# Making the masks and decays of retention on the chip as outer products, with a new order of the work

## The chip, the core and the metric

One core of a Trainium2 chip runs one program. The core's engines are TensorE (PE, matmuls; PEld is its loading of weights), VectorE (DVE), ScalarE (ACT), GpSimd (POOL) and SyncE (SP, which here issues every DMA). Each runs its own instructions in order and waits on semaphores for the others. The metric is the time of one execution on the device in microseconds (us), the median of several runs; lower is better.

## What is computed

```python
def _attn_ref(q, k, v):                      # q, k, v: (4, 8, 576, 64) float32
    scores = scale * np.matmul(q, k.transpose(0, 1, 3, 2))
    gamma = 1.0 - 2.0 ** (-5.0 - np.arange(H, dtype=np.float32))
    rel = pos[:, None] - pos[None, :]
    Dmat = np.where(rel >= 0, gamma[:, None, None] ** rel[None, :, :], 0.0)
    return np.matmul(scores * Dmat[None, :, :, :], v)

def _moe_ref(x, w_in, w_out):                # x: (2304, 512), d_ff = 2048
    h = x @ w_in
    return (h * np.cos(h)) @ w_out

def _moe2_ref(x, w_in, w_out):
    h = x @ w_in
    return (np.maximum(h, 0.0) + np.log1p(np.exp(-np.abs(h)))) @ w_out
```

Retention (attention with a decay `gamma ** (distance)` per head in place of a softmax), then two dense layers with different activations. Scale is 1/8.

## The kernel before

**Retention.** A sequence of 576 tokens is cut into a first part of 256 and a second of 320. One *piece* is one part of one batch for one pair of heads: 32 pieces. A piece's raw tile `raw` holds queries, keys and values. PE makes the scores of two 128-token blocks (`scores`, line 615) into a set of two PSUM banks (`s`/`o`, `acc0`/`acc1`, `acc2`/`acc3`, `ha`/`hb` in turn), DVE multiplies them by the mask `m_t` (line 642, `p<-s`), POOL scales the keys by `dk_t` (line 585) and the queries by `dq_t` (line 592, `qs`), PE sums keys times values (`sums`, line 620) to a state `st`, and two pieces later PE adds the masked and the carried part (`back`, line 692). `m_t` has a 128x128 triangle per head, `dq_t` a decay by position, `mt_t` the masks of the last 64 tokens. All three were computed on the host and are loaded, as is the small `dk_t`. ACT and DVE then split the result in a high and a low part (`x`, lines 727 and 308).

**The layers.** Every fp32 factor is split in two reduced-precision parts, `gh`/`gl`, `wh`/`wl`, and three products are summed. Weights come as 64-bit words (`wr`) and are rebuilt by ACT (`wy`, `wr`, lines 363 and 369) and DVE (`wk`, lines 375 to 386) before they are split into `wh` and `wl` (line 431 and the helper of line 308). The first 8 of 16 column blocks `f` of layer 1 run in groups of 512 or 384 tokens (lines 779 and 883). From about 278 us on the rest of layer 1 and layer 2 run as a Strassen-like scheme (lines 921 and 1001), in which `tt`, `pair`, `cv` and `x` are sums and differences of blocks.

**What sets the order.** Every operation is given to `Plan.op` with an engine, an estimated duration, a key (a wished time) and its dependences. `Plan.order` then lists them by a model of engines, ports and the DMA link; the model's times decide the order of each engine's instructions, and for operations that may run on two engines (`POOL_DVE`, `ACT_DVE`) also which. Nothing of these times is kept on the chip: only the order and the data's semaphores count. The first 16 pieces (`4 * ALONE`) come alone, the others between matmuls of the first three groups. Ahead of piece 0 and after pieces 0 and 1 PE runs filling matmuls on zeros (`warm`, `fill`, line 1053; `FILL = (2, 5)`).

Of the kernel before, what the change touches and what calls it, by code (L numbers as in the profile page):

```python
# [7 lines left out]
F32 = mybir.dt.float32  # L8
# [46 lines left out]
def t_pool(n):  # L55
    return n * 0.00228 + 0.06
# [9 lines left out]
    return layer == 2 or f < FA  # L66


FLEX = 0.317
FLEX_AD = 0.993  # L70
FLEX_2 = 50.0
ROOM = 258.786
SPARE = 0.082
LATE = 3.0
NP = 3
RS = 5
WR = 3
GB = 2
PT = 3
R0 = 22.0  # L80
WB = (21.627, 3.294)
W2 = (31.803, 7.371, 15.278, -5.922)
W3 = (30.221, 11.772, 18.502)
XC = 9.717
LAG_C = 1.399
LAG_S = 0.9
TT = 3
CA = (-2.626, 2.436, 6.269, 13.332)
TURN = 0.6
XS = 61.276  # L90
FILL = (2, 5)
EARLY = 2.474
EARLY_2 = 5.754
AHEAD = {}
GAP = 2.0
LO_A = "pool or dve"
END = 3.1
LC = 2.5
LL = 3.862
LB = 1.9  # L100
WARM = 350
DX = 20.621
LEAD = 7.302
W0 = (40.929, 1.68, 3.451)
M0 = 28.434
AK = (1.0, 2.2)
# [8 lines left out]
TIE = -0.21
LAG = -2.133
LEAD_G = 7.197
CX = 0.278
# [5 lines left out]
class Plan:  # L124
# [29 lines left out]
    def order(self):  # L154
        n = len(self.ops)
        behind, loose = [set() for _ in range(n)], set()
        for bufs, made in self.rings.values():
            for k, (i, _) in enumerate(made):
                if k:
                    behind[i].add(made[k - 1][0])  # L160
                if k >= bufs:
                    self.ops[i][4].update(self.users.get(made[k - bufs][1], ()))
            for i, tile_key in made:
                for u in self.users.get(tile_key, ()):
                    if u != i:
                        if i not in self.ops[u][4]:
                            loose.add((u, i))
                        self.ops[u][4].add(i)
        for i, o in enumerate(self.ops):
            o[4].discard(i)  # L170
            behind[i].discard(i)
            behind[i] -= o[4]
        after = [[] for _ in range(n)]
        next_ = [[] for _ in range(n)]
        left = [0] * n
        for i, o in enumerate(self.ops):
            left[i] = len(o[4]) + len(behind[i])
            for d in behind[i]:
                next_[d].append(i)
            for d in o[4]:  # L180
                after[d].append(i)
        ready = [0.0] * n
        free, port, link = dict.fromkeys(("pe", "act", "dve", "pool", "sp", "host"), 0.0), 0.0, 0.0
        can = [i for i in range(n) if not left[i]]
        start, end, self.eng = [0.0] * n, [0.0] * n, [None] * n
        window, busy, warm = 0, 0.0, False
        for _ in range(n):
            best = None
            for i in can:
                eng, dur, key, _, _, uses_port, _ = self.ops[i]  # L190
                if eng == POOL_DVE:
                    f = max(ready[i], port)
                    t, d, e = min(
                        ((max(f, free[e]), d, e) for e, d in (("pool", t_pool(dur)), ("dve", t_dve(dur)))),
                        key=lambda o: o[0] + (FLEX if ready[i] < ROOM else FLEX_2) * o[1])
                elif eng == ACT_DVE:
                    t, d, e = min(
                        ((max(ready[i], free[e], port if e == "dve" and uses_port else 0.0), d, e) for e, d in zip(("act", "dve"), dur)),
                        key=lambda o: o[0] + FLEX_AD * o[1] + (SPARE if o[2] == "dve" else 0.0))
                else:  # L200
                    t, d, e = max(free[eng], ready[i], port if uses_port else 0.0, key - LEAD if eng == "sp" else 0.0), dur, eng
# [53 lines left out]


@with_exitstack
def retention_moe_moe(ctx, tc, qkv, w1, w2, mask, mtail, dq, dk, out):
    nc = tc.nc
    pool = lambda name, bufs=1, **kw: ctx.enter_context(tc.tile_pool(name=name, bufs=bufs, **kw))  # L260
    dram = pool("dram", space=bass.MemoryType.DRAM)
# [269 lines left out]
    def front(i, K):  # L531
# [99 lines left out]
    def masks(i, K):  # L631
# [225 lines left out]
    def parts(e, src, r, n, i, K2, in_psum):  # L857
# [211 lines left out]
    HT = ("ha", "hb", "s", "o")

# [254 lines left out]
```

## Time and profile before

| | us |
|---|---|
| median of 3 runs | 858.13 (857.58 to 859.51) |
| the profiled execution | 857.71 |
| its span, first to last instruction | 855.9 |
| PE busy | 842.1 (98%) |
| DVE busy | 653.2 (76%) |
| ACT busy | 480.0 (56%) |
| POOL busy | 53.2 (6%) |

The profiled execution's own time is 1.8 us longer than its span. PE's matmuls overlap in the pipeline, so a busy PE need not be at its peak. An idle engine costs time only where another waits for it.

### The profile page before, as it was taken

Reading aid. Unit: us, or ns where it says so; the run is one execution under the profiler, and the core shown is the slowest. Engines: PE = TensorE matmul, PEld = TensorE weight load, DVE = VectorE, ACT = ScalarE, POOL = GpSimd, SP = SyncE. Lnnn points to the kernel's source line nnn. Section 1 sums busy time; section 2 is a strip of 40 time slices with the busy share of each in tenths; the row PEclk is TensorE's granted clock in tenths of the full one; section 3 lists DMA queues with packets and bytes.
Section 4 is the critical chain, followed back from the end, with each engine's and each line's share of the span. In section 5 each row is a group of like instructions: output and inputs, shape, how many; then the busy total and the mean of one; then the engine's idle time right before and its main releaser. Section 6 shows DMA issues by size and latency. Waiting matters only on the chain.

```text
span 855.9 us, 13829 instructions
## 1 busy us (share of the span) xinstructions
PE 842.1 (98%) x5084; PEld 756.9 (88%) x5084; DVE 653.2 (76%) x1281; ACT 480.0 (56%) x951; POOL 53.2 (6%) x73
## 2 busy tenths in 40 slices
PE   7989999999999999999999999999999999999998
PEld 5767777899988899999999998898998988989986
DVE  3889987776799898778899898588669665655653
ACT  1378654746676776556777575466547533333331
POOL 3630100100121000000000000000000000000000
PEclk9999999999999999999999999999999999999999
DMA  8876779654784132332377658357456454252203
GB/s 311 343 264 202 268 260 353 204 198 157 257 289 157 52 124 95 128 126 80 122 261 263 227 187 331 127 216 273 160 196 227 173 194 158 75 181 78 74 1 111
DMA packets 66852, 160.56 MB, mean 188 GB/s; under 512 B 6240, under 2 KB 26336, under 8 KB 66784
## 3 DMA queue, kind: packets, MB, share of 16 engines
q1 hardware_dynamic: 66784, 159.68, 53.2%
q8 instruction: 40, 0.66, 0.3%
q14 instruction: 28, 0.23, 0.1%
HBM read 104.34 MB, written 55.31 MB: 187 GB/s over the span
## 4 chain that ended last, share of the span: by engine, by line
PE 86%; DVE 7%; ACT 3%; issue 1%; DMA 1%; SPq 0%; POOL 0%; DVEq 0%; POOLq 0%; ACTq 0%
PE acc L1001 34%; PE ha L921 17%; PE acc L883 9%; PE s L921 8%; PE hb L921 4%; PE ha L779 4%; PE hb L779 3%; PE o L692 2%; PE s L615 1%; DVE tt L1175 1%; DVE wk L382 1%; PE s L779 1%; PE s L620 1%; DMA dq_t<-in_dq 1%; DVE gl L308 1%
## 5 line engine op out<-in xcount | busy, mean ns | idle before, releaser
L1001 PE MATMUL acc<-pair,gh 128*128 128x512 f32 x576 | 178.5, 391 | 0.0
L921 PE MATMUL ha<-x,pair 128*128 128x384 f32 x864 | 174.3, 336 | 0.0
L921 PEld LDWEIGHTS ha<-x,pair 128*128 128x128 f32 x864 | 152.6, 188 | 5.1 <-DVE g L831 0.3
L308 DVE TENSOR_TENSOR gl<-g,gh 128x384 fp32r<-128x384 f32 x144 | 79.6, 554 | 66.6 <-ACT gh L862 66.0
L862 ACT ACTIVATE gh<-g 128x384 fp32r<-128x384 f32 x144 | 74.8, 521 | 92.1 <-PE acc L1001 88.4
L1001 PEld LDWEIGHTS acc<-pair,gh 128*128 128x128 f32 x576 | 107.3, 188 | 19.0
L1001 PE MATMUL acc<-pair,gl 128*128 128x512 f32 x288 | 113.3, 393 | 0.0
L1001 PE MATMUL acc<-gh,pair 128*128 128x384 f32 x384 | 105.1, 334 | 0.0
L845 ACT ACTIVATE er<-er 128x384 f32<-128x384 f32 x96 | 50.3, 524 | 73.5 <-DVE er L842 73.0
L921 PE MATMUL s<-x,pair 128*128 128x384 f32 x432 | 86.8, 335 | 0.9 <-DVE gl L308 0.9
L921 PEld LDWEIGHTS s<-x,pair 128*128 128x128 f32 x432 | 75.9, 188 | 1.5 <-DVE gl L308 1.2
L1001 PEld LDWEIGHTS acc<-gh,pair 128*128 128x128 f32 x384 | 70.1, 188 | 0.0
L1001 PE MATMUL acc<-gl,pair 128*128 128x384 f32 x192 | 64.5, 336 | 1.1 <-DVE gl L308 1.1
L828 ACT ACTIVATE er<-er,hp_t 128x384 f32<-128x384 f32 (+1 forms) x88 | 56.3, 643 | 15.5 <-DVE er L825 14.2
L1001 PEld LDWEIGHTS acc<-pair,gl 128*128 128x128 f32 x288 | 54.0, 188 | 11.4
L883 PE MATMUL acc<-gh,wh 128*128 128x512 f32 (+1 forms) x160 | 60.3, 377 | 0.3 <-ACT gh L862 0.3
L883 PE MATMUL acc<-gl,wh 128*128 128x512 f32 (+1 forms) x160 | 59.3, 370 | 0.8 <-DVE gl L308 0.7
L883 PE MATMUL acc<-gh,wl 128*128 128x512 f32 (+1 forms) x160 | 59.0, 369 | 0.0
L363 ACT ACTIVATE wy<-wr 128x512 f32<-128x512 f32 x64 | 42.6, 666 | 9.8 <-DVE wk L382 8.2
L382 DVE SCALAR_TENSOR_TENSOR wk<-wy,wk 128x512 int32<-128x512 int32 x64 | 46.0, 718 | 0.8
L312 ACT ACTIVATE cv<-ha 128x384 f32<-128x384 f32 x67 | 32.9, 491 | 23.5 <-PE ha L921 21.7
L921 PE MATMUL hb<-x,pair 128*128 128x384 f32 x216 | 43.8, 337 | 0.0
(180 smaller groups left out, 1507.7 us busy)
## 6 DMA issues: line engine op xcount, KB each, us to landing
wr<-in_w SPq DMA_DIRECT2D x64, 512.0 KB, 4.5
sd<-x SPq DMA_DIRECT2D x21, 768.0 KB, 4.2
x<-sd SPq DMA_DIRECT2D x21, 768.0 KB, 7.2
wd<-wk SPq DMA_DIRECT2D x40, 256.0 KB, 2.8
wr<-wd SPq DMA_DIRECT2D x20, 512.0 KB, 4.5
raw<-in_qkv SPq DMA_DIRECT2D x12, 640.0 KB, 6.1
raw<-in_qkv SPq DMA_DIRECT2D x12, 512.0 KB, 5.7
x<-xdh SPq DMA_DIRECT2D x12, 384.0 KB, 4.7
```

Source lines behind the costliest of these rows:

```text
L308: e.tensor_tensor(out_, a, hi.bitcast(F32), ALU.subtract)
L312: nc.scalar.activation(out_, in_, AF.Copy)
L363: nc.scalar.activation(y, T["wr", u][:, :, 1].bitcast(F32), AF.Copy, scale=2.0 ** -112)
L382: nc.vector.scalar_tensor_tensor(a, T["wy", u], -(1 << 31), a, ALU.bitwise_and, ALU.bitwise_or)
L692: nc.tensor.matmul(o_at(z)[Z[j]], lhs(j), rhs(j), start=start, stop=stop, skip_group_check=True)
L779: nc.tensor.matmul(h_[:, 0:n], lhs, rhs[:, d, 0:n], start=(k == 0), stop=(k == 3 * NC - 1))
L828: nc.scalar.activation(e["r"], e["r"], AF.Sin, bias=hp_t[:, 0:1], scale=-1.0)
L845: nc.scalar.activation(e["r"], e["r"], AF.Softplus)
L862: nc.scalar.activation(e["gh"], src(), AF.Copy)
L883: nc.tensor.matmul(acc[o][:, 0:n], l[:, s], e[r], start=(first and z == 0), stop=(last and z == 2))
L921: nc.tensor.matmul(R(r), w_(a), x_(b), start=(start and n == 0), stop=(n == 5), skip_group_check=True)
L1001: nc.tensor.matmul(acc[m] if ph else acc[m][:, 0:HN], l, r, start=(first and z == 0), stop=(last and z == 2))
```

## The change

The tables `mask`, `mtail` and `dq` are no longer inputs. In their place come `decay`, 8 rows (one per head) of 1664 numbers, and `causal`, a 128x128 square of ones and zeros. Row `h` of `decay` holds `gamma_h ** -s` in the columns of head `h`, ones in another column range, and `gamma_h ** t / 8`. PE multiplies them (contraction over 8 rows): the first by the last gives `gamma ** (t - s) / 8`, which DVE multiplies by `causal` into `m_t`; the ones by the last give the decay by position, which ACT copies to `dq_t`; ACT copies `mt_t` out of `m_t`. The tiles of the table lie where a weight block comes later, the products in PSUM banks of pieces 2 and 3. Besides, most keys of the plan have new values, the model's DMA link has other constants before 60 us, a third rule for the choice of POOL or DVE holds from 655 us on, and one operation (`gl` outside PSUM) counts as a user of the port that DVE and POOL share.

```diff
-FLEX = 0.317
-FLEX_AD = 0.993
+FLEX = 0.464
+FLEX_AD = 1.483
...
+SOON = 60.0
+FLEX_3 = 0.5
+ROOM_3 = 655.0
...
-KK = 2.915
-KQ = 0.903
+KK = -2.954
+KQ = -28.538
...
-                        key=lambda o: o[0] + (FLEX if ready[i] < ROOM else FLEX_2) * o[1])
+                        key=lambda o: o[0] + (FLEX if ready[i] < ROOM else FLEX_2 if ready[i] < ROOM_3 else FLEX_3) * o[1])
...
-                link = max(link, t + 1.7) + nbytes / 365e3
-                end[i] = link + (0.95 if t < 60.0 else LATE)
+                if t < SOON:
+                    link = max(link, t + 2.0) + nbytes / 405e3
+                    end[i] = link + 0.7
+                else:
+                    link = max(link, t + 1.7) + nbytes / 365e3
+                    end[i] = link + LATE
...
-        op("dve", t_dve(n), K2 + 0.5, g2, r=r + [gh_k], w=[gl_k], new=[("gl", GB, gl_k[0])])
+        op("dve", t_dve(n), K2 + 0.5, g2, r=r + [gh_k], w=[gl_k], new=[("gl", GB, gl_k[0])], port=not in_psum)
...
+    dma(lambda: T["dec"][0][0:8], lambda: decay[:, 0:1024], 8 * 4096, K - 2.0, w=[(("dec", 0), 0)], new=[("w0", 1, ("dec", 0))], pre=dec_tiles)
+    dma(lambda: T["dec"][1][0:8, 0:640], lambda: decay[:, 1024:1664], 8 * 2560, K - 1.9, r=[(("dec", 0), 0)], w=[(("dec", 0), 1)])
+    dma(lambda: T["dec"][1][:, 640:768], lambda: causal, 128 * 512, K - 1.8, r=[(("dec", 0), 0)], w=[(("dec", 0), 2)])
...
+    def outer_m(hp):
+        if hp % 2 == 0:
+            T["om", hp // 2] = bank(("acc2", "acc3")[hp // 2])
+        for j in range(2):
+            a = (hp % 2 * 2 + j) * 128
+            nc.tensor.matmul(T["om", hp // 2][:, a:a + 128], T["dec"][0][0:8, (2 * hp + j) * 128:(2 * hp + j) * 128 + 128], rows_(), start=True, stop=True)
+
+    def outer_q():
+        T["oq"] = bank("ha")
+        for hp in range(4):
+            nc.tensor.matmul(T["oq"][:, hp * 128:hp * 128 + 128], T["dec"][1][0:8, hp * 128:hp * 128 + 128], rows_(), start=True, stop=True)
+
+    def cut_m(hp):
+        nc.vector.tensor_tensor(
+            m_t[:, hp], T["om", hp // 2][:, hp % 2 * 256:hp % 2 * 256 + 256].rearrange("p (a s) -> p a s", a=2),
+            T["dec"][1][:, 640:768].rearrange("p (a s) -> p a s", a=1).to_broadcast([128, 2, 128]), ALU.mult)
+
     for hp in range(4):
-        K = AK[0] - DX + 2.0 * hp
-        dma(lambda hp=hp: m_t[:, hp], lambda hp=hp: mask[:, hp], 128 * 1024, K, w=[("cst", "m", hp)])
-        if hp == 0:
-            dma(lambda: dk_t, lambda: dk, 128 * 48, K + 0.1, w=[("cst", "k")])
-            dma(lambda: dq_t[:, :, 0:128], lambda: dq[:, :, 0:128], 128 * 2048, K + 0.2, w=[("cst", "q")])
-    dma(lambda: dq_t[:, :, 128:320], lambda: dq[:, :, 128:320], 128 * 3072, AK[0] - DX + 9.0, w=[("cst", "q2")])
-    dma(lambda: mt_t, lambda: mtail, 128 * 1024, AK[0] - DX + 9.1, w=[("cst", "t")])
+        ok = (("om", hp // 2), hp % 2)
+        op("pe", 2 * t_mm32(128), K + 0.1 * hp, lambda hp=hp: outer_m(hp), r=dec_k, w=[ok], new=[(("acc2", "acc3")[hp // 2], 1, ok[0])] if hp % 2 == 0 else [])
+        op("dve", t_dve(256), K + 0.5 + hp, lambda hp=hp: cut_m(hp), r=[ok, (("dec", 0), 2)], w=[("cst", "m", hp)])
+    op("pe", 4 * t_mm32(128), K + 0.15, outer_q, r=dec_k, w=[(("oq",),)], new=[("ha", 1, ("oq",))])
...
```

Three places of the order follow. Line numbers of the changed kernel are 7 higher or more; a number behind `acc` names one PSUM tile.

PE near its start, before: the scores of piece 1 (`acc_159`, `acc_160`), the sums of piece 0 (`s`), five filling matmuls (`hb<-er`), the scores of piece 2.

```order
L615 MATMUL acc_159<-raw 128x128
L615 MATMUL acc_160<-raw 128x128
L620 MATMUL s<-raw 64x64 x4
L1053 MATMUL hb<-er 128x128 x5
L615 MATMUL acc_192<-raw 128x128
```

And of the change, where `dec` is the table:

```order
L622 MATMUL acc_153<-raw 128x128
L622 MATMUL acc_154<-raw 128x128
L627 MATMUL s<-raw 64x64 x4
L1084 MATMUL acc_167<-dec 128x128 x4
L1089 MATMUL ha<-dec 128x128 x4
L1084 MATMUL acc_190<-dec 128x128 x4
L1060 MATMUL hb<-er 128x128 x5
L622 MATMUL acc_221<-raw 128x128
```

Twelve matmuls stand between the sums of piece 0 and the filling matmuls, where nothing stood.

DVE about the end of the 16 pieces, before: splits of piece 13 (`x<-acc_159`), two weight halves (`wk`), a key scaling (`raw`), the low part of a weight (`wl`), and state and masks of piece 16 (`st`, `p`).

```order
L308 TENSOR_TENSOR x<-acc_159,x 128x64
L375 SCALAR_TENSOR_TENSOR wk<-wy,wr 128x512
L382 SCALAR_TENSOR_TENSOR wk<-wy,wk 128x512
L585 TENSOR_TENSOR raw<-raw,dk_t 128x256
L375 SCALAR_TENSOR_TENSOR wk<-wy,wr 128x512
L308 TENSOR_TENSOR wl<-wk,wh 128x512
L674 SCALAR_TENSOR_TENSOR st<-st,dk_t,s 128x64
L642 TENSOR_TENSOR p<-s,m_t 128x256
L642 TENSOR_TENSOR p<-o,m_t 128x256
```

And of the change:

```order
L315 TENSOR_TENSOR x<-acc_153,x 128x64
L382 SCALAR_TENSOR_TENSOR wk<-wy,wr 128x512
L389 SCALAR_TENSOR_TENSOR wk<-wy,wk 128x512
L592 TENSOR_TENSOR raw<-raw,dk_t 128x256
L382 SCALAR_TENSOR_TENSOR wk<-wy,wr 128x512
L649 TENSOR_TENSOR p<-s,m_t 128x256
L681 SCALAR_TENSOR_TENSOR st<-st,dk_t,s 128x64
L649 TENSOR_TENSOR p<-o,m_t 128x256
```

The `wl` row is gone from DVE (POOL has one more), and the state stands behind the first mask.

DVE at the end of the groups of layer 1 (its slots `hb`, `s` and `o`, with the first Strassen-like inputs `tt` and `x` between them), before:

```order
L831 TENSOR_TENSOR hb<-hb,er 128x512
L308 TENSOR_TENSOR x<-tt,x 128x768
L818 SCALAR_TENSOR_TENSOR er<-ek,s 128x512
L1175 TENSOR_TENSOR tt<-x 128x768
L1175 TENSOR_TENSOR tt<-tt 128x768
L831 TENSOR_TENSOR s<-s,er 128x512
L308 TENSOR_TENSOR gl<-hb,gh 128x512
L818 SCALAR_TENSOR_TENSOR er<-ek,o 128x512
L825 TENSOR_SCALAR er<-er 128x512
L831 TENSOR_TENSOR o<-o,er 128x512
L308 TENSOR_TENSOR gl<-s,gh 128x512
```

And of the change, from the row behind `hb<-hb,er` and one `pair` row on:

```order
L1216 TENSOR_TENSOR tt<-tt 128x768
L825 SCALAR_TENSOR_TENSOR er<-ek,s 128x512
L1216 TENSOR_TENSOR tt<-tt 128x768
L315 TENSOR_TENSOR x<-tt,x 128x768
L838 TENSOR_TENSOR s<-s,er 128x512
L315 TENSOR_TENSOR gl<-hb,gh 128x512
L1216 TENSOR_TENSOR tt<-x 128x768
L1216 TENSOR_TENSOR tt<-tt 128x768
L825 SCALAR_TENSOR_TENSOR er<-ek,o 128x512
L832 TENSOR_SCALAR er<-er 128x512
L838 TENSOR_TENSOR o<-o,er 128x512
L315 TENSOR_TENSOR gl<-s,gh 128x512
```

Two `tt` rows now stand between `gl<-hb` and `gl<-s`; before, none did.

## Rows read from the trace of the kernel before

**Rows 1.** The page: busy us by engine, and the chain that ended last.

```profile
PE 842.1 (98%) x5084; PEld 756.9 (88%) x5084; DVE 653.2 (76%) x1281; ACT 480.0 (56%) x951; POOL 53.2 (6%) x73
...
PE 86%; DVE 7%; ACT 3%; issue 1%; DMA 1%; SPq 0%; POOL 0%; DVEq 0%; POOLq 0%; ACTq 0%
```

**Rows 2.** Windows: us, PE, PEld, DVE, ACT, POOL busy, clock, DMA share, GB/s.

```profile
10.00:20.00 10.00, 7.72 (x124) 5.95 (x124) 4.77 (x16) 1.82 (x6) 4.72 (x8) 1.00 1.05 383
40.00:50.00 10.00, 7.45 (x122) 6.19 (x120) 9.44 (x32) 7.25 (x22) 4.72 (x6) 0.93 0.81 264
50.00:60.00 10.00, 9.67 (x73) 7.23 (x73) 7.78 (x16) 7.11 (x14) 3.06 (x4) 0.90 0.84 281
60.00:90.00 30.00, 29.22 (x168) 22.73 (x168) 28.15 (x51) 25.06 (x46) 3.25 (x4) 1.00 0.62 199
90.00:160.00 70.00, 70.00 (x477) 55.84 (x474) 59.00 (x126) 41.33 (x79) 7.11 (x10) 1.00 0.77 275
260.00:345.00 85.00, 83.01 (x434) 76.10 (x433) 78.01 (x139) 58.58 (x114) 2.03 (x1) 1.00 0.32 107
```

**Rows 3.** PE's waits: total us, times, longest; first 0:60, then from 60 us.

```profile
PE s L615 <- ACT x L727: 2.5, 1, 2.5
PE acc L620 <- POOL raw L585: 2.0, 1, 2.0
...
PE acc L615 <- DMA raw<-in_qkv: 0.9, 2, 0.6
...
PE acc L1001 <- DVE gl L308: 1.1, 2, 0.8
PE s L921 <- DVE gl L308: 0.9, 1, 0.9
```

**Rows 4.** DMA issues up to 24 us: count, KB each, median us to landing.

```profile
m_t<-in_mask SPq DMA_DIRECT2D x4, 128.0 KB, 4.6
dq_t<-in_dq SPq DMA_DIRECT2D x1, 384.0 KB, 5.6
```

**Rows 5.** Windows of the loading, columns as in group 2.

```profile
8.00:20.00 12.00, 9.52 (x144) 7.56 (x146) 5.48 (x18) 2.04 (x7) 5.92 (x11) 1.00 1.05 377
20.00:38.00 18.00, 18.00 (x308) 13.95 (x304) 13.72 (x47) 5.79 (x19) 11.46 (x20) 1.00 1.01 400
```

**Rows 6.** Timeline of the head: start, duration, engine, line, operation.

```profile
4.43 0.43 SPq L300 DMA_DIRECT2D m_t<-in_mask  x1
6.51 0.42 DVE L642 TENSOR_TENSOR p<-s,m_t 128x256 f32<-128x256 f32 x1 [5.11 <-PE o L615]
6.85 0.41 DVE L642 TENSOR_TENSOR p<-o,m_t 128x256 f32<-128x256 f32 x1
9.22 1.38 PE L1053 MATMUL hb<-er 128*128 128x128 f32 x10
10.53 0.71 PE L615 MATMUL acc<-raw 64*128 64x128 f32 x8
19.45 0.45 PE L620 MATMUL acc<-raw 128*64 128x64 f32 x8 [1.98 <-POOL raw L585]
20.75 0.71 PE L615 MATMUL acc<-raw 64*128 64x128 f32 x8
```

**Rows 7.** Timeline around PE's stop at 45.7 us.

```profile
46.75 1.10 DVE L308 TENSOR_TENSOR wl<-wk,wh 128x512 fp32r<-128x512 f32 x1
47.97 0.41 DVE L642 TENSOR_TENSOR p<-s,m_t 128x256 f32<-128x256 f32 x1
...
48.48 0.64 PE L615 MATMUL s<-raw 64*128 64x128 f32 x2 [2.55 <-ACT x L727]
```

**Rows 8.** Windows behind that stop, columns as in group 2.

```profile
48.00:50.00 2.00, 1.52 (x10) 1.32 (x12) 2.00 (x10) 0.67 (x1) 0.16 (x1) 0.66 0.82 258
50.00:52.00 2.00, 2.00 (x20) 1.35 (x20) 0.79 (x2) 0.85 (x2) 0.90 (x1) 0.50 0.90 287
```

**Rows 9.** Timeline: one combination ahead of the wait at 281 us.

```profile
274.89 0.95 DVE L1175 TENSOR_TENSOR tt<-x 128x768 f32<-128x768 f32 x1
```

More of the change, by code (lines that the diff above doesn't have):

```diff
@@ L79 @@
 PT = 3
[L80 to L84, printed above, removed]
+R0 = 21.479
+WB = (5.156, 1.056)
+W2 = (31.803, 10.357, 15.057, 1.575)
+W3 = (30.906, 9.432, 20.743)
+XC = 9.86
 LAG_C = 1.399
@@ L87 @@
 TT = 3
-CA = (-2.626, 2.436, 6.269, 13.332)
+CA = (1.351, 2.377, 6.269, 14.268)
 TURN = 0.6
-XS = 61.276
+XS = 61.277
 FILL = (2, 5)
-EARLY = 2.474
-EARLY_2 = 5.754
+EARLY = 0.052
+EARLY_2 = 9.429
 AHEAD = {}
@@ L98 @@
 LC = 2.5
-LL = 3.862
-LB = 1.9
+LL = 3.772
+LB = 0.338
 WARM = 350
[L102 to L106, printed above, removed]
+DX = 20.689
+LEAD = 7.249
+W0 = (41.07, 1.68, 7.082)
+M0 = 28.193
+AK = (1.15, 1.458)
 PAIR_A = 1.107
@@ L112 @@
 SCALE = "pool"
-KK = 2.915
-KQ = 0.903
[L115 to L118, printed above, removed]
+KK = -2.954
+KQ = -28.538
+TIE = -1.013
+LAG = -2.776
+LEAD_G = 7.59
+CX = 0.971
 GT = (3, 4)
@@ L257, in retention_moe_moe @@
 @with_exitstack
-def retention_moe_moe(ctx, tc, qkv, w1, w2, mask, mtail, dq, dk, out):
+def retention_moe_moe(ctx, tc, qkv, w1, w2, decay, causal, dk, out):
     nc = tc.nc
@@ L595, in front @@
         op(scale_eng, 256 if scale_eng == POOL_DVE else t_pool(256), K - KK, scale_k if scale_eng == POOL_DVE else lambda: scale_k(nc.gpsimd), r=[vk, ("cst", "k")], w=[kk], port=True)
-        op(scale_eng, nq if scale_eng == POOL_DVE else t_pool(nq), K - KQ, scale_q if scale_eng == POOL_DVE else lambda: scale_q(nc.gpsimd), r=[rk, ("cst", "q")] + ([("cst", "q2")] if c else []), w=[qk], new=[("qs", QS, qk[0])], port=True)
+        op(scale_eng, nq if scale_eng == POOL_DVE else t_pool(nq), K - KQ, scale_q if scale_eng == POOL_DVE else lambda: scale_q(nc.gpsimd), r=[rk] + [("cst", "q", z) for z in range(3 if c else 1)], w=[qk], new=[("qs", QS, qk[0])], port=True)
         st["qk"] = qk
@@ L656, in mask_tail @@
                 nc.vector.tensor_tensor(st["dp"], X()[0][:, at_t], mt_t[:, hp], ALU.mult)
-            op("dve", t_dve(64), K + 0.1, mask_tail, r=[xt, ("cst", "t")], w=[d_k], new=[("dp", 3, d_k[0])])
+            op("dve", t_dve(64), K + 0.1, mask_tail, r=[xt, ("cst", "t", 0), ("cst", "t", 1)], w=[d_k], new=[("dp", 3, d_k[0])])
             st["pk"].append(d_k)
@@ L1067, in retention_moe_moe, with dec_tiles @@
-    dma(lambda: mt_t, lambda: mtail, 128 * 1024, AK[0] - DX + 9.1, w=[("cst", "t")])
+    K = AK[0] - DX
+    def dec_tiles():
+        T["dec"] = wa_of(0).tile([128, 1024], F32, tag="wh0", name="dec"), wa_of(0).tile([128, 1024], F32, tag="wl0", name="dec")
+    dma(lambda: T["dec"][0][0:8], lambda: decay[:, 0:1024], 8 * 4096, K - 2.0, w=[(("dec", 0), 0)], new=[("w0", 1, ("dec", 0))], pre=dec_tiles)
+    dma(lambda: T["dec"][1][0:8, 0:640], lambda: decay[:, 1024:1664], 8 * 2560, K - 1.9, r=[(("dec", 0), 0)], w=[(("dec", 0), 1)])
@@ new lines, in retention_moe_moe @@
+    dma(lambda: T["dec"][1][:, 640:768], lambda: causal, 128 * 512, K - 1.8, r=[(("dec", 0), 0)], w=[(("dec", 0), 2)])
+    dma(lambda: dk_t, lambda: dk, 128 * 48, K + 0.1, w=[("cst", "k")])
+    rows_ = lambda: T["dec"][1][0:8, 512:640]
+    dec_k = [(("dec", 0), 0), (("dec", 0), 1)]
+    def outer_m(hp):
[4 more added lines that the diff above has]
+            nc.tensor.matmul(T["om", hp // 2][:, a:a + 128], T["dec"][0][0:8, (2 * hp + j) * 128:(2 * hp + j) * 128 + 128], rows_(), start=True, stop=True)
@@ new lines, in retention_moe_moe @@
+    for hp in range(4):
+        ok = (("om", hp // 2), hp % 2)
+        op("pe", 2 * t_mm32(128), K + 0.1 * hp, lambda hp=hp: outer_m(hp), r=dec_k, w=[ok], new=[(("acc2", "acc3")[hp // 2], 1, ok[0])] if hp % 2 == 0 else [])
+        op("dve", t_dve(256), K + 0.5 + hp, lambda hp=hp: cut_m(hp), r=[ok, (("dec", 0), 2)], w=[("cst", "m", hp)])
+    op("pe", 4 * t_mm32(128), K + 0.15, outer_q, r=dec_k, w=[(("oq",),)], new=[("ha", 1, ("oq",))])
+    oq = lambda n: T["oq"].rearrange("p (h s) -> p h s", h=4)[:, :, 0:n]
@@ new lines, in retention_moe_moe @@
+    for z, (a, n) in enumerate(((0, 128), (128, 128), (256, 64))):
+        op("act", t_act(4 * n, True), K + 1.0 + 3 * z, lambda a=a, n=n: nc.scalar.activation(dq_t[:, :, a:a + n], oq(n), AF.Copy), r=[(("oq",),)],
+           w=[("cst", "q", z)])
+    for j in range(2):
+        z = slice(64 * j, 64 * j + 64)
+        op("act", t_act(256), K + 8.0 + j, lambda j=j, z=z: nc.scalar.activation(mt_t[z], m_t[z, :, j, z], AF.Copy),
+           r=[("cst", "m", hp) for hp in range(4)], w=[("cst", "t", j)])
@@ L1294 @@
     pos = np.arange(128, dtype=np.float64)
-    heads = gam.reshape(4, 2)
-    rel = pos[None, :] - pos[:, None]
-    mask = np.where(rel >= 0, gam[:, None, None] ** np.maximum(rel, 0), 0.0) * 0.125
-    mtail = np.concatenate([mask[0::2, :64, :64], mask[1::2, :64, :64]], axis=1).transpose(1, 0, 2)
-    mask = mask.reshape(4, 2, 128, 128).transpose(2, 0, 1, 3)
-    by_row = np.repeat(heads.T, 64, axis=0)
-    dq = by_row[:, :, None] ** (np.arange(320) % 128)[None, None, :] * 0.125
+    heads = np.arange(H)
+    up = np.zeros((H, H, 128))
+    up[heads, heads] = gam[:, None] ** -pos
+    pick = np.zeros((H, H, 64))
+    pick[heads, heads] = 1.0
+    decay = np.concatenate([up.reshape(H, -1), pick.reshape(H, -1), gam[:, None] ** pos * 0.125], axis=1)
+    causal = pos[None, :] >= pos[:, None]
+    by_row = np.repeat(gam.reshape(4, 2).T, 64, axis=0)
     dk = np.concatenate([gam[None, :] ** (128 - pos[:, None]), by_row ** 128], axis=1)
@@ L1307 @@
         w2=w_layout(inputs["moe2_w_in"], inputs["moe2_w_out"]),
-        mask=mask.astype(np.float32),
-        mtail=mtail.astype(np.float32),
-        dq=dq.astype(np.float32),
+        decay=decay.astype(np.float32),
+        causal=causal.astype(np.float32),
         dk=dk[..., None].astype(np.float32),
```

## The prediction

> **What bounds the kernel now.** I read the page first: TensorE (PE) is busy 98% of the span and holds 86% of the chain that ended last [rows 1], so only time in which PE waits or runs slowly can be won. The windows by stage say where that is [rows 2]. From 90 to 160 us PE is never idle. It loses 2.3 of 10 us in 10:20, 2.6 in 40:50, 0.8 of 30 in 60:90 and 2.0 of 85 in 260:345. Two of these stretches are set by VectorE (DVE), which is busy 28.15 of 30 us in 60:90 and 78.01 of 85 in 260:345. The list of PE's waits names what ended them [rows 3]: up to 60 us the masks (released late, 2.5, shown as a wait behind ACT's evictions), a scaled key tile on POOL (2.0) and raw loads (0.9 in two waits, 0.6 and 0.3); after 60 us 3.0 us in all, nearly all for the low part `gl`. All else is work that the change does not touch: no matmul of the two MoE layers is removed.
>
> **The loads and what takes their place.** `m_t` (4 x 128 KB) and `dq_t` (384 KB [rows 4], and 256 by the diff), and `mt_t` (128 by the diff), go: 1.31 million bytes in all. The table is 8 x 6656 bytes and the causal square 64 KB, 0.12 million together. Bytes from HBM move at 377 to 400 GB/s from 8 to 38 us, with the DMA engines at a share of 1.0 [rows 5], so the raw loads behind the tables come 1.19 million / 390 thousand per us = 3 us sooner. That removes the waits on raw loads and on the scaled key (2.0 + 0.9 us), which hung on a late raw tile.
>
> But PE has to make the tables itself before piece 2, where it did not have to before. The 12 outer products are fp32, 128 columns, and stand on PE between the sums of piece 0 and the five filling matmuls, which the change leaves in place. The nearest row is those five: they start at 9.22 and the next work starts at 10.53 [rows 6], 0.26 us each. Twelve take 3.1 us. That the outer products fill 8 rows of the array and not 128 is no row of before; I take no saving from it, and the bounds are 2.6 us (if the change of work between kinds, paid once, is a third of the 1.31) and 3.1. Piece 1 starts 0.6 sooner, because its load wait goes. So piece 2 starts at 10.53 - 0.6 + 3.1 = 13.0. DVE's four cuts by the causal square look like its mask rows, which start 0.34 apart [rows 6]. From the first outer products at about 9.2, DVE has four cuts and four masks to start until the last cut is through: 8 x 0.34 = 2.7, so 11.9, and piece 2's PSUM banks are free about 1 us before PE wants them. From piece 2 to piece 6 before took 20.75 - 10.53 = 10.2 us, of which 2.3 were the waits that go; 7.9 stay, and piece 6 starts at 20.9, where it started at 20.75. **The head gains nothing: term 0**, bounds -0.5 (outer products at 2.6) and +1.0 (below). All 3 us of saved loading are spent on PE. From 20 to 38 us PE is busy without a gap [rows 5], so earlier raw tiles bring nothing there either.
>
> The table has to be there by 8.6 us, when PE is through with piece 0's sums (9.22 less the 0.6 of piece 1). Its second part is the eighth DMA issued. The eighth DMA of before was issued at 4.43 [rows 6], and the loads of this kind took 4.6 (`m_t`) to 5.6 us (`dq_t`) to land [rows 4], so 9.0 to 10.0; with 390 KB fewer bytes ahead of it, 1 us less, 8.0 to 9.0. I take no wait; the bound is +1.0 us.
> The Trainium skill (DMA: Bandwidth & Descriptors, Rules for kernel authors) speaks against a table of 8 rows: an outermost dimension under 16 confines a DMA to that many of the 16 engines. No run here shows such a transfer yet; by that rule the 32 KB and 20 KB would load at half the engines' rate, still under half a us by the 390 GB/s of the rows, which leaves the sum as it is.
>
> ACT's five copies (three for `dq_t`, two for `mt_t`) lie where ACT is busy 1.82 of 10 us [rows 2]: hidden. Without that cover the state copies queue behind them, a us at most.
>
> **The stop at 45.7 us.** After piece 16 PE stands 2.55 us until 48.48 [rows 7], until DVE has made the masks `p<-s` of piece 16 (start 47.97). Ahead of them on DVE stand `wl` (46.75, 1.10 us) and a short state row. The order of the changed kernel hands this `wl` to POOL (busy 4.72 of 10 us in 40:50 [rows 2], so there is room; without it the weight half, not wanted before the second f, would be late) and puts the state behind the first mask; the mask follows the `wk` row directly. `wk` ended just ahead of 46.8, so the mask can start 1.1 us sooner. Against it: ACT now makes `wy` and two `wr` after three evictions and not before them, so the first `wk` of this place waits where it did not; I charge 0.1. **Term -1.0**, bounds 0 and -1.2.
>
> **The clock.** Behind this stop PE's granted clock is 0.66 in 48:50 and 0.50 in 50:52 [rows 8], so about 0.68 x 2.0 + 2.0 = 3.4 us at the lower level of 1.2 GHz; at 2.4 the same work takes 1.7 us less. A pause of 2.0 us before 19.45 [rows 6] left the clock at 1.00 [rows 5]; the one of 2.55 did not. The new pause is 2.55 - 1.0 = 1.5, on the safe side of both. **Term -1.7**, bounds 0 and -1.7.
> The Trainium skill (TensorE: Matmul & The Clock Gate, What's actually happening) says that the gate goes by how busy PE has been lately; by that rule the other pauses nearby count too, so a pause of 1.5 us is no promise. That is the first rival.
>
> **What is given back.** PE then enters MoE 2.7 us sooner, but until 85 us DVE paces it (28.15 of 30 us busy). DVE itself comes only 1.0 us sooner to this place, and has 0.6 + 2.2 us idle in 40:60 to fill [rows 2]; I let it close a third of that, 0.7. In 60:90 the plan moves one key scaling and some absolute values from POOL and ACT to DVE and some `wl` the other way, about level. So 1.7 of 2.7 arrive at 90 us: **term +1.0**, bounds 0 and +2.7.
>
> **From 260 to 345 us**, DVE paces PE once more, with 2.0 us of waits [rows 3]. Of this place the order shows that two `tt` combinations and a `pair` row of the Strassen-like stage move from ahead of `hb<-hb,er` to behind it, two of them between `gl<-hb` and `gl<-s`, the row for which PE waits 0.9 at 281 us. A `tt` lasts 0.95 [rows 9]: up to 1.9 us more at this wait, if DVE does not come to the place sooner. Elsewhere the new order may end both waits (-2.0). The row between is the wait itself, so I take **0**, bounds -2.0 and +1.9 at this one place. From 345 us on PE is never short; the last units keep their order.
>
> **The sum.** 0 - 1.0 - 1.7 + 1.0 + 0 = -1.7. The profiled execution of before took 857.71 us, of which 855.9 are the span; it lies 0.42 under the median of 858.13. So 856.0 for a like execution and **856.4** for the median. A measurement of this kernel can tell about 0.2%, 1.7 us, from no change; the forecast lies just there.
>
> **Rivals.** (1) The clock drops all the same, because the pause is still long enough or the next wait on the masks adds to it. Then PE comes 1.0 sooner, DVE closes 0.2 less: -0.9, 857.2, no change to be told. For it: both pauses known are near the new one. Chance 0.20. (2) The outer products come late: the table lands at 10 us or the copies run longer than the rows they are like, +1.0 in the head, which passes on to 45 us; -0.7, 857.4. Chance 0.13. (3) **Slower:** in 260 to 345 us DVE has more to do before each `gl`. It is idle only 7 of 85 us in 260:345 [rows 2], and the new keys put weight rows in other places on it. If two places like the one at 281 lose their 1.9 us in full and the gain of the head only fills in DVE's wait, the net is +3.8 - 1.7 = +2.1, 860.2; it decides from a delay of 3.4 us on. For it: the order at `gl<-s`; against it: 2.0 us of PE's waits there could go too. Chance 0.21. (4) Faster still: DVE is not the limit in 60:90, so nothing is given back, and the waits of 260 to 345 go: -1.0 - 1.7 - 2.0 = -4.7, 853.4. Chance 0.12. That the change only swaps loads for work on idle engines, and nothing else happens, is inside (1) and (2).
>
> **Numbers.** The forecast has 0.34. Faster: 0.34 + 0.12 = 0.46. Same: 0.20 + 0.13 = 0.33. Slower: 0.21. The range runs from 853.4 (rival 4) to 859.6 (most of rival 3 short of its full price); I leave about 0.1 above it and 0.08 below.
>
> **What would show it.** Head: twelve outer products of 2.6 to 3.1 us in all near 8.6, piece 2 at 13.0, piece 6 at 20.9, no wait on raw loads. Stop: `p<-s` of piece 16 near 46.9 and PE back at about 47.4, granted clock 1.00 in 48:52. Layer 1: DVE at least 28 of 30 us in 60:90. At 281: PE's wait for `gl` between 0 and 2.8. Wrong would be the forecast if piece 6 starts by 18.5 (then the head does gain what it saves in loads), or if PE's waits of 260 to 345 sum to over 5 us.

## The result

The changed kernel takes 864.35 us (median of 20 runs, 859.61 to 867.15); the kernel before took 858.55 beside it (median of 20). The ratio is 1.0058, with a 95% interval of 1.0046 to 1.0071: the change made the kernel slower by 5 us, where I had forecast 1.7 us less, and the time lies above the range. (The two medians differ by 5.8 us; the ratio is that of the means, 863.98 to 858.96, and leaves out one far slower execution of the kernel before, of 922.65 us.) Its profiled execution took 862.54 us (span 860.8), 4.8 more than that of before.

Two lists of PE's waits of the changed kernel, up to 60 us and from 60 us on (total us, times, longest; some rows left out), to be read against [rows 3]:

```profile
PE s L622 <- ACT x L734: 2.0, 1, 2.0
...
PE acc L1084 <- DMA dec<-in_causal: 0.4, 1, 0.4
...
PE s L928 <- DVE gl L315: 3.7, 1, 3.7
PE acc L890 <- DVE gl L315: 0.7, 1, 0.7
...
PE hb L928 <- DVE gl L315: 0.4, 1, 0.4
```

The waits on raw loads and on the scaled key are gone, as they should. The stop at the end of the 16 pieces went from 2.5 to 2.0 only, and the wait for `gl` at the start of the Strassen-like stage from 0.9 to 3.7. The windows (columns as in [rows 2]) against [rows 2]:

```profile
10.00:20.00 10.00, 10.00 (x123) 8.07 (x121) 5.65 (x18) 3.99 (x11) 5.99 (x11) 0.83 1.03 401
40.00:50.00 10.00, 8.02 (x146) 6.73 (x147) 8.88 (x34) 6.67 (x21) 4.34 (x5) 0.98 0.86 309
50.00:60.00 10.00, 9.89 (x68) 7.26 (x65) 8.06 (x18) 6.41 (x12) 2.79 (x3) 0.84 0.75 277
60.00:90.00 30.00, 29.15 (x162) 22.53 (x162) 29.22 (x52) 25.84 (x48) 2.38 (x3) 1.00 0.62 199
260.00:345.00 85.00, 80.48 (x415) 74.47 (x414) 77.16 (x134) 57.07 (x109) 6.40 (x3) 0.98 0.31 106
```

PE is now busy for all of 10:20, but at a clock of 0.83 where it had 1.00; 260:345 has lost 2.5 us of PE's busy time, and its clock is 0.98. Where the 4.8 us arose can be dated: the first matmul of line 928 (921 before) starts at 278.08 us, and started at 278.06. Up to there the two executions are level. The loss comes in the next 11 us. The timeline of the changed kernel there, DVE and then PE:

```profile
278.94 0.68 DVE L315 TENSOR_TENSOR gl<-hb,gh 128x512 fp32r<-128x512 f32 x1
279.53 0.95 DVE L1216 TENSOR_TENSOR tt<-x 128x768 f32<-128x768 f32 x1
280.52 0.96 DVE L1216 TENSOR_TENSOR tt<-tt 128x768 f32<-128x768 f32 x1
...
283.93 0.68 DVE L315 TENSOR_TENSOR gl<-s,gh 128x512 fp32r<-128x512 f32 x1
...
278.08 1.23 PE L928 MATMUL ha<-x,pair 128*128 128x384 f32 x6
...
284.66 1.84 PE L928 MATMUL s<-x,pair 128*128 128x384 f32 x6 [3.66 <-DVE gl L315]
```

And of the kernel before, in the same order:

```profile
277.35 0.68 DVE L308 TENSOR_TENSOR gl<-hb,gh 128x512 fp32r<-128x512 f32 x1
...
280.49 0.68 DVE L308 TENSOR_TENSOR gl<-s,gh 128x512 fp32r<-128x512 f32 x1
...
278.06 1.23 PE L921 MATMUL ha<-x,pair 128*128 128x384 f32 x6
...
281.23 1.33 PE L921 MATMUL s<-x,pair 128*128 128x384 f32 x6 [0.90 <-DVE gl L308]
```

So DVE comes to this place 1.6 us late, and the two `tt` rows add 1.86 (279.53 to 281.39). PE stands 3.66 us, and then runs slowly (windows behind the wait):

```profile
284.00:286.00 2.00, 1.34 (x6) 1.34 (x7) 2.00 (x5) 1.97 (x3) 0.00 (x0) 0.80 0.00 0
286.00:288.00 2.00, 2.00 (x6) 1.62 (x5) 1.83 (x4) 0.87 (x2) 0.00 (x0) 0.50 0.00 0
288.00:290.00 2.00, 2.00 (x9) 1.64 (x8) 2.00 (x4) 1.14 (x2) 0.00 (x0) 0.84 0.00 0
```

At 1.00 these six us would have done (0.20 + 0.50 + 0.16) x 2 = 1.7 us more. Before, the clock was 1.00 in them. The wait is 2.8 longer than before, the clock costs 1.7, together 4.5 of the 4.8; a wait of 0.4 for `gl<-hb`, in the list above, is new as well. Behind this stretch smaller waits come (1.4 us in all) and go (1.1).

The same loss of clock stands right behind the outer products. The timeline of PE there, and the windows:

```profile
8.03 1.12 PE L1084 MATMUL acc<-dec 8*128 8x128 f32 x8 [0.38 <-DMA dec<-in_causal]
9.00 1.05 PE L1089 MATMUL ha<-dec 8*128 8x128 f32 x8
9.89 1.05 PE L1084 MATMUL acc<-dec 8*128 8x128 f32 x8
10.87 1.38 PE L1060 MATMUL hb<-er 128*128 128x128 f32 x10
12.19 1.23 PE L622 MATMUL acc<-raw 64*128 64x128 f32 x8
```

```profile
10.00:12.00 2.00, 2.00 (x19) 1.88 (x17) 1.98 (x6) 1.36 (x3) 0.62 (x1) 1.00 1.02 392
12.00:14.00 2.00, 2.00 (x23) 1.66 (x23) 0.07 (x1) 0.83 (x2) 1.96 (x5) 0.54 1.03 403
14.00:16.00 2.00, 2.00 (x26) 1.46 (x24) 1.23 (x4) 0.58 (x3) 1.12 (x3) 0.61 1.05 403
```

PE has no gap from 8.03 us on, and still its clock goes to the lower level of 1.2 GHz in 12:14. Before, it was 1.00 throughout [rows 5].

### The profile page after: what moved, and what is told of

It is laid out like the page before. It is cut to its first block, busy times and chain, and to the rows that moved or that the text cites. A ratio compares the mean times of both kernels' runs of the same rounds, so it can differ in the third digit from the quotient of the medians.

```text
span 860.8 us, 13893 instructions
## 1 busy us (share of the span) xinstructions
PE 846.7 (98%) x5108; PEld 761.6 (88%) x5108; DVE 658.0 (76%) x1294; ACT 478.9 (56%) x946; POOL 57.0 (7%) x74
## 4 chain that ended last, share of the span: by engine, by line
PE 84%; DVE 9%; ACT 4%; issue 1%; DMA 1%; SPq 0%; DVEq 0%; ACTq 0%
PE acc L1008 33%; PE ha L928 16%; PE acc L890 8%; PE s L928 8%; PE hb L928 4%; PE ha L786 3%; PE hb L786 3%; PE o L699 2%; PE s L622 1%; DVE wk L389 1%; DVE gl L315 1%; DVE er L825 1%; DVE tt L1216 1%; PE acc L699 1%; PE s L627 1%
```

## Experiments

All times are medians, of 10 runs (new_keys 7, rows_128 5, masks_first 4, the change 20). The ratios are to the kernel before in runs on the same chip, and they decide, since the chips differ: its median was 859.51 us beside the four kernels from old_keys on, 859.14 beside the next four, 858.98 beside the last four. A ratio is not the quotient of the two medians. The low clock is a property of the execution, so the executions of one kernel spread with it: of the 20 of the changed kernel the fastest, 859.61 us, had a mean clock of 0.998, the slowest, 867.15, one of 0.987. Differences under 1 us between two kernels mean little for that reason.

| kernel | us | ratio to before, 95% interval | clock 8:20 us |
|---|---|---|---|
| the change | 864.35 | 1.0058 (1.0046 to 1.0071) | 0.86 |
| old_keys | 860.67 | 1.0005 (0.9988 to 1.0022) | 0.72 |
| new_keys | 863.77 | 1.0052 (1.0025 to 1.0080) | 1.00 |
| low_first | 861.96 | 1.0022 (1.0005 to 1.0039) | 0.86 |
| masks_first | 864.92 | 1.0053 (1.0034 to 1.0072) | 0.72 |
| rows_128 | 861.20 | 1.0035 (1.0022 to 1.0049) | 1.00 |
| tt_on_dve | 860.75 | 1.0018 (1.0000 to 1.0037) | 0.72 |
| all_three | 857.04 | 0.9973 (0.9961 to 0.9985) | 1.00 |
| old_128 | 857.92 | 0.9994 (0.9984 to 1.0005) | 1.00 |
| more_8 | 861.64 | 1.0022 (1.0007 to 1.0036) | 0.59 |
| more_128 | 858.54 | 0.9993 (0.9978 to 1.0009) | 1.00 |
| all_four | 856.58 | 0.9977 (0.9964 to 0.9990) | 1.00 |
| three_no_fill | 856.82 | 0.9976 (0.9965 to 0.9987) | 1.00 |

**old_keys and new_keys: which half of the change loses.** In the first the outer products stay and the plan is as before; in the second the tables are loaded and the plan is new.

```diff
 # old_keys: the changed kernel with before's constants, link model, rule for POOL or DVE, and port flag
-FLEX = 0.464
+FLEX = 0.317
...
 # new_keys: the kernel before with the change's
-FLEX = 0.317
+FLEX = 0.464
...
```

> The outer products with every key and every constant of the plan's model as before. Theory A (the loss is the new order's: the wait of 3.7 us for the low part at 281 us and the low clock behind it, while the tables cost about what they save): the wait at 281 us is back under 1.5 us, and the time is 857 to 860. Theory B (the outer products lose it: a low clock behind them at 12 us, and what follows): as after, 862 to 866.

> The tables loaded as before, with the new keys and model constants. Theory A (the loss is the new order's): 861 to 865, with a wait of over 2.5 us for the low part near 281 us. Theory B (the outer products lose it): 857 to 860, and the granted clock is 1.00 from 8 to 45 us.

The order loses; of the outer products no loss can be told from the times: with the old keys they are at 1.0005, and the interval leaves room for 1.9 us; with the new keys and no outer products it is 1.0052. The profiled executions, cut at the first matmul of line 928, are sharper. From there to the end the kernel before takes 577.8 us, the change 582.7, old_keys 578.1, new_keys 582.1: the 4 to 5 us behind that row belong to the order. Up to it the four take 278.1, 278.1, 280.8 and 279.9: old_keys loses 2.7 us there, and new_keys 1.8 (among its waits is one of 2.1 for `x` on DVE, ahead of piece 6). The wait for `gl` near 282 us is 0.4 with the old keys, and is there without the outer products (PE's waits of new_keys, 260 to 345 us), if shorter than the 2.5 us I had named:

```profile
PE s L928 <- DVE gl L315: 2.1, 1, 2.1
```

So theory B was half true as well. Its second sign, the clock, is in the windows 8:20: old_keys, and new_keys behind it.

```profile
8.00:20.00 12.00, 11.45 (x106) 9.95 (x106) 5.10 (x15) 3.39 (x10) 5.25 (x10) 0.72 1.01 379
```

```profile
8.00:20.00 12.00, 10.35 (x152) 7.82 (x148) 5.02 (x16) 2.21 (x8) 4.55 (x8) 1.00 1.03 367
```

The low clock at 12 us goes with the outer products, whatever the plan.

**low_first: the two rows at 281 us.** The emitted order is the plan's, with two operations moved.

```diff
 # the two tt, behind gl<-s
+MOVES = [([1335, 1336], 1062)]
...
-        for i in self.order():
+        order = self.order()
+        for some, anchor in MOVES:
+            order = [i for i in order if i not in some]
+            at = order.index(anchor) + 1
+            order[at:at] = some
+        for i in order:
```

> The changed kernel with only the two combinations (tt) at 279.5 and 280.5 us moved behind the low part gl<-s at 281 us. Theory A (these two rows and the low clock are the loss): the wait of 3.7 us falls by the two rows' 1.9 to about 1.8, the clock stays at 1.00 there, and the time falls by 1.9 + 1.7 = 3.6 us to about 860.8. Rival (DVE is late as a whole, and the two rows only wait elsewhere): another wait of about 2 us shows up by 310 us, and the time falls by at most 1.7 us, to 862.6 or more.

PE's waits from 60 us on:

```profile
PE s L934 <- DVE gl L321: 1.8, 1, 1.8
PE ha L934 <- ACT cv L325: 0.9, 1, 0.9
```

And the window 280:290:

```profile
280.00:290.00 10.00, 7.50 (x36) 6.36 (x36) 9.14 (x16) 6.17 (x11) 0.00 (x0) 1.00 0.01 2
```

The wait fell to the 1.8 expected and the clock is 1.00 in 280:290. The new wait of 0.9, at 289 us, is what the rival foresaw, at half its size. The ratio falls from 1.0058 to 1.0022, by 3.1 us; each such difference of two ratios is known to some 2 us. That is nearer to theory A (3.6) than to its rival (1.7 at most), but does not decide: in the profiled execution the way from line 928 to the end is 580.8 us, only 1.9 less than the change's.

**tt_on_dve: why DVE is late.** Only the engine of four operations differs.

```diff
 # tt of 257.6 to 268.9 us, POOL's by the plan
+ON_DVE = [1322, 1323, 1324, 1325]
...
+        order = self.order()
+        for i in ON_DVE:
+            self.eng[i] = "dve"
```

> The changed kernel with the four combinations (tt) that POOL makes from 257.6 to 268.9 us put on DVE, at 0.87 us each, in the same place of the order. Theory A (POOL's work at the port that it shares with DVE holds DVE up by 1.65, 1.64, 1.64 and 0.47 us, and makes gl<-s late): DVE gains 5.4 and pays 3.5, the wait of 3.7 us at 281 us falls to about 1.8, and with the clock at 1.00 there the time falls by up to 3.6 us against the changed kernel. Rival (the long rows of DVE are not POOL's doing): DVE has 3.5 us more to do, the wait grows to about 7 us, and the time rises by over 3 us.

In the changed kernel, DVE's and POOL's rows of that time read as follows.

```profile
262.42 1.95 POOL L1216 TENSOR_TENSOR tt<-x 128x768 f32<-128x768 f32 x1 [2.83 <-DVE pair L315]
264.46 2.17 POOL L1216 TENSOR_TENSOR tt<-tt 128x768 f32<-128x768 f32 x1
...
262.60 2.33 DVE L315 TENSOR_TENSOR pair<-tt,pair 128x512 fp32r<-128x512 f32 x1
264.85 2.33 DVE L389 SCALAR_TENSOR_TENSOR wk<-wy,wk 128x512 int32<-128x512 int32 x1
```

DVE rows of this size take 0.68 us (`gl<-hb` above); these take 2.33, and the first ends 0.56 us after POOL's `tt` (264.93 against 264.37): it ran when POOL was through. Before, POOL made three such `tt`, from 253.56 on, and DVE had three long rows beside them (2.06, 1.26 and 2.33 us, 3.9 more than these rows take alone); now it makes four, nearer to the wait, and DVE loses 5.4. With POOL's four on DVE the `pair` row is short, `gl<-hb` starts at 277.17 instead of 278.94, and PE's wait is 2.0:

```profile
262.39 0.68 DVE L324 TENSOR_TENSOR pair<-tt,pair 128x512 fp32r<-128x512 f32 x1
...
277.17 0.68 DVE L324 TENSOR_TENSOR gl<-hb,gh 128x512 fp32r<-128x512 f32 x1
```

```profile
PE s L937 <- DVE gl L324: 2.0, 1, 2.0
```

So handing a `tt` to the idle POOL costs DVE up to 1.7 us of standing (the four cost 1.66, 1.65, 1.64 and 0.47) where doing it itself costs 0.87. The ratio is 1.0018: 3.4 us less than the change, as theory A has it and against the rise that its rival asked for, though in the profiled execution the clock was still 0.83 in 280:290 and the way from line 928 to the end 580.3 us, 2.4 less than the change's. The Trainium skill (SBUF — State Buffer, SBUF: two separate sides) says why: a DVE instruction with two inputs in SBUF and a POOL instruction that reads SBUF share a port pair, which one of them holds for its whole instruction while the other is blocked. The trace agrees, 2.33 against 0.68 us.

**masks_first: what the stop at 46 us is worth.**

```diff
 # st<-s of piece 16 on ACT right behind its sums; p<-s, st and p<-o on DVE ahead of the weight halves; loop as in low_first
+MOVES = [([343], 340), ([341, 344, 342], 223)]
```

> The changed kernel with the masks and the state of piece 16 put on DVE ahead of the weight halves that stand there, and the state's first copy on ACT ahead of the weight copies. Theory A (up to 85 us DVE paces, so time won at this stop is given back): PE's stop of 2.0 us at 46.7 us and the low clock behind it go, PE enters the first layer up to 3.7 us sooner, but is at most 1 us ahead at 90 us: 863.3 to 864.4. Rival (the stop is paid in full): 3.7 us, so about 860.7.

PE's waits of this kernel from 44 to 62 us have no stop before the scores of piece 17 any more:

```profile
PE ha L792 <- DVE x L321: 1.3, 1, 1.3
PE acc L896 <- ACT gh L875: 1.0, 1, 1.0
```

And 1.0 more for `gl` a little later. In the changed kernel the waits of that stretch are 2.0, 0.7 and 0.2, 2.9 in all; here 3.3. The stop is not paid: it moves to the first weights and the first `gh` and `gl` of layer 1. The ratio of 1.0053 (four runs) is that of the change. This profiled execution had a lower clock at 12 us, and piece 6 at 23.74 where the change has 21.48, so its waits are not like for like; all_four below repeats the edit at a clock of 1.00.

**rows_128, more_8 and more_128: the clock behind the outer products.** In rows_128 the table's tiles are zeroed first and all 128 rows multiplied; the first part of the table is issued behind five other loads (at 3.17 us, not at 0.74), so that DVE has time for the zeros. The other two are the kernel before, loaded tables and all, with twelve filling matmuls more at the same place of PE's order.

```diff
 # rows_128
+MOVES = [([4], 32)]
...
+        nc.vector.memset(T["dec"][1][:, 0:640], 0.0)
+        nc.vector.memset(T["dec"][0], 0.0)
...
-    rows_ = lambda: T["dec"][1][0:8, 512:640]
+    rows_ = lambda: T["dec"][1][:, 512:640]
...
 # more_8 (MORE = 8) and more_128 (MORE = 128)
-lambda i=i: fill(128, FILL[i])
+lambda i=i: ([fill(128, 1, MORE) for _ in range(12 * i)], fill(128, FILL[i]))
```

> The changed kernel with the two tiles of the table zeroed on DVE beforehand and the outer products taken over 128 rows, of which 120 are zero; the first part of the table is issued four loads later, to give DVE time. Same products, same columns. Theory A (the low clock from 12 to 15 us comes of matmuls that fill 8 rows): the granted clock is 1.00 from 8 to 20 us, piece 2 to piece 6 take 7.9 us where they took 9.3, and if that time is not given back before 90 us the median is 1.7 us below the changed kernel's. Rival (it comes of what goes before or behind, whatever the rows): the clock falls to 0.5 again near 12 us, and the time is that of the changed kernel.

> The kernel before with twelve more filling matmuls of 128 columns over 8 rows of zeros, at the place where the change has its outer products; nothing else differs, the tables are loaded. Theory A (matmuls over 8 rows bring the clock down): the granted clock is below 0.9 in 8:20 us, as in the changed kernel, and piece 6 starts at 21 us or later. Rival (the low clock comes from the change's other edits at the front): the clock is 1.00 in 8:20.

> The same twelve matmuls over 128 rows of zeros. Theory A: the clock is 1.00 in 8:20 us, and the time is 1 to 2 us below that with 8 rows, unless it is given back before 90 us. Rival: no difference between 8 and 128 rows in the clock of 8:20 or in the time.

The windows 8:20 of rows_128, more_8 and more_128, in that order:

```profile
8.00:20.00 12.00, 11.78 (x162) 10.01 (x162) 7.46 (x24) 4.01 (x11) 6.16 (x12) 1.00 1.01 388
```

```profile
8.00:20.00 12.00, 11.68 (x86) 10.39 (x86) 1.97 (x7) 0.67 (x3) 2.94 (x6) 0.59 1.03 375
```

```profile
8.00:20.00 12.00, 11.39 (x160) 9.53 (x156) 5.48 (x18) 2.05 (x7) 5.59 (x9) 1.00 1.02 369
```

The same twelve matmuls, on the same zeros, bring the clock to 0.59 over 8 rows and leave it at 1.00 over 128. With 128 rows they cost nothing (0.9993), with 8 the ratio is 1.0022: 861.64 against 858.54 us, 3.1 us. In the profiled executions line 928 starts at 278.1 with 128 rows and at 283.5 with 8. In the changed kernel 128 rows bring piece 6 from 21.48 to 20.17 us, line 928 from 278.08 to 276.05, and the ratio from 1.0058 to 1.0035, 2.0 us. Theory A holds in all three. A pause just ahead is not the cause: rows_128 waits 0.7 us there and keeps its clock, the change 0.4 and loses it. All six profiles with matmuls over 8 rows have a clock of 0.59 to 0.86 in 8:20, all eight without them (that of before among them) 1.00.

**all_three and old_128: the losses together, and the outer products alone.** all_three has the edits of low_first, tt_on_dve and rows_128; old_128 those of old_keys and rows_128.

> The changed kernel with three edits: the two combinations behind gl<-s, the four combinations of POOL on DVE, and the outer products over 128 rows. If the three losses are apart from each other: the wait at 281 us is under 1 us, the clock falls at one place at most (near 50 us), and the time is 5 us below the changed kernel's, at the kernel before or up to 1 us below it. If what is won at the front is given back by 90 us and the wait moves on behind 281 us, it stays 2 us above that.

> The outer products over 128 rows, with every key of the plan as before. Theory A (without the low clock at 12 us the outer products win what they save in loads, and it lasts): 1.5 to 2.5 us below the kernel before. Rival (DVE paces PE up to 85 us, and gives it back): within 0.7 us of the kernel before.

all_three is 0.9973, 2.3 us under the kernel before and 7.3 under the change; it beats both, and by more than I had named (1 and 5). From line 928 to the end it takes 578.4 us. PE's waits from 60 us on no longer have the wait at 281 us; the largest is the one that came up behind it:

```profile
PE ha L937 <- ACT cv L328: 0.9, 1, 0.9
...
PE acc L899 <- DVE gl L324: 0.5, 1, 0.5
```

One by one the edits win 3.1, 3.4 and 2.0 us, 8.5 in all; the first two both shorten the same wait. old_128 decides for its rival: 0.9994. The outer products win 0.7 us at piece 6 (20.08 against 20.75), and nothing by line 928 (278.17 against 278.06) or at the end.

**all_four and three_no_fill: is more to be had?** all_four adds the edit of masks_first, three_no_fill takes the five filling matmuls out of all_three (`fill(128, FILL[i]) if i == 0 else None`).

> The kernel with the three edits, and the masks and the state of piece 16 ahead of the weight halves as well. If DVE paces PE up to 85 us, PE's stop of 2.0 us at 45 us goes and the time stays within 1 us of the three edits' (2.1 us under the kernel before); if the stop and the low clock behind it are paid in full, it falls by another 2 to 3.7 us.

> The kernel with the three edits, without the five filling matmuls behind the outer products (1.3 us of PE before piece 2). If they only take time there: pieces 2 to 15 start 1.3 us sooner, and after what is given back by 90 us the time falls by up to 0.7 us. If they keep the clock up, or the masks and raw tiles are not there sooner: PE waits at piece 2, the clock falls in 10:20, and the time is the same or up to 1.7 us longer.

Neither differs from all_three (0.9977 and 0.9976). Without the stop at 45 us PE waits 1.3, 0.9 and 0.7 us in 47 to 59 instead: given back once more. The profiled execution of all_four reaches piece 6 at 20.50 and line 928 at 276.44; three_no_fill, which keeps the stop, at 20.55 and 276.48. Without the filling matmuls PE waits 0.9 us at piece 2 for the table's cut on DVE, and the clock in 8:20 stays at 1.00.

## Why the prediction was wrong

**What bounds the kernel** stood: only PE's waits and its clock moved the time, and nearly all that moved it lies in the four places named. Between the forecast for the profiled execution (-1.7) and its time (+4.8) lie 6.5 us: 1.7 ahead of line 928, where the gain did not come, and 4.8 behind it, where the forecast had 0.

**The head: "term 0, bounds -0.5 and +1.0".** The table came 0.38 us late for PE, within the bound of 1.0. The outer products took 2.84 us (8.03 to 10.87), inside the bounds of 2.6 to 3.1 (the lower one, 3.1 less a third of 1.31, should read 2.7), and piece 2 came at 12.19, sooner than the 13.0 forecast. The way from piece 2 to piece 6 was to be 7.9; it is 8.0 with 128 rows (12.18 to 20.17) and 9.3 in the change, so piece 6 started at 21.48 and not at 20.9. The term lacked the clock, which no sentence of that part asked about. In rows_128 line 928 starts at 276.05, 2.0 us earlier than before: without the low clock the front gained about what the forecast gave it, though not by the steps that it named. Of the six profiled executions with 8 rows the changed kernel's is one of the two mildest: in the others piece 6 starts at 22.21, 23.74, 24.28 and 23.99, and in more_8 at 25.99. That fits the median of the change, which lies 1.8 us over its own profiled execution; part of the lateness in these five is a later table, by 0.7 to 1.1 us in four of them.

In the forecast I used the Trainium skill (TensorE: Matmul & The Clock Gate, What's actually happening), by which the gate goes by how busy PE has been lately. Here the trace differs, if busy means that matmuls run without a gap: PE was busy 2.00 of 2.00 us in 10:12 and got 0.54 in 12:14, and 8 or 128 rows made the difference.

**The stop: "-1.0, bounds 0 and -1.2".** It fell by 0.56, and PE was back at 48.65, not at 47.4. Two things failed in that step. The state was moved behind the first mask, but it reads the same bank `s` that PE wants, so the bank came free no sooner; and the `wk` row ahead of both, which I had ending just before 46.8, waited for ACT, charged at 0.1. The timeline of the changed kernel:

```profile
46.58 0.66 ACT L370 ACTIVATE wy<-wr 128x512 f32<-128x512 f32 x1 [0.98 <-DVE wk L389]
...
47.33 0.69 DVE L382 SCALAR_TENSOR_TENSOR wk<-wy,wr 128x512 int32<-128x512 int32 x1 [0.51 <-issue]
...
47.94 0.42 DVE L649 TENSOR_TENSOR p<-s,m_t 128x256 f32<-128x256 f32 x1
...
48.27 0.27 DVE L681 SCALAR_TENSOR_TENSOR st<-st,dk_t,s 128x64 f32<-128x64 f32 x1
...
48.65 0.34 PE L622 MATMUL s<-raw 64*128 64x128 f32 x1 [1.99 <-ACT x L734]
```

ACT's `wy` ends at 47.24, `wk` starts, the mask follows, then the state (to 48.54), and then PE. The list of waits names ACT's `x` there; the state is as near to PE's start, and in new_keys the list names it.

**The clock: "-1.7, bounds 0 and -1.7".** Nothing came of it: the clock was 0.92 in 48:50 and 0.84 in 50:60, and the time lost in 48:60 is 1.7 us, as before. The bounds took the length of the one pause as what decides. In old_keys a wait of 2.0 us at the same stop left the clock at 1.00 in 50:60; in the change one of 2.0 did not. What decides it stays open. This was the first rival, given 0.20.

**Given back: "+1.0".** The kind is shown by masks_first and all_four; PE entered layer 1 at 51.60 where it had 52.01, so 0.4 us were there to give back, and piece 20 starts 0.36 later than before (88.50 against 88.14). But not all is given back: the 1.3 us that rows_128 wins at piece 6 are 2.0 at line 928.

**260 to 345 us: "0, bounds -2.0 and +1.9 at this one place".** This is the step that made the sign wrong. Rival 3 had the mechanism and the place, and asked for 3.4 us from two such places; one gave 4.5. My sign of it, waits of over 5 us in 260 to 345, did not come: they sum to 4.6, because the sign counted waits and not the clock behind them. The upper bound counted the two `tt` rows alone. It left out that DVE could come there late, since no step of the sum priced what DVE loses beside POOL; and it left out the clock behind a longer wait, though [rows 8] had priced just that elsewhere. tt_on_dve shows POOL's share in the delay: without the four `tt` on POOL `gl<-hb` starts 1.8 us sooner, more than the 1.6 by which it was late. Against the kernel before, POOL's share grew by 1.5 us (5.4 against 3.9), less the 0.87 of one `tt` that DVE no longer makes. What is left fits weight work that is done later (DVE is busy 62.44 us in 160:245, before 64.37, and 14.84 in 245:260, before 13.20), but that was not tried by itself.

## What to carry to other kernels

A matmul that fills few rows of the array can cost more than its own time (3.1 us between more_8 and more_128): look at the granted clock behind it, and pad the contraction with zero rows where that is cheap, as here. Work given to an idle POOL is not free while DVE paces the kernel; price it by the long DVE rows that stand beside POOL's. And a wait has two prices, its length and the 1.7 us of slow clock that may follow, so an order should be judged at the one place where the late operand is wanted, with what runs ahead of it on the engine, rather than by sums over a stage.

## What the runs showed of the hardware

The granted clock fell although PE was busy without a gap: with twelve matmuls over 8 rows to 0.59 in 8:20 us, with the same twelve over 128 rows it stayed at 1.00. And the clock differs from execution to execution of one program: its mean went from 0.987 to 0.998 over the 20 runs of the change, and the time from 867.15 to 859.61 us.
